# Reordering the first transfers and the first TensorE work of a one-core attention-and-MLP backward kernel, and leaving out fifteen marker loads

## The chip, the cores and the metric

The kernel runs on one core of one Trainium2 chip. The metric is the device time of one execution in microseconds (us). The time before is the median of three runs. A separate, profiled execution of the same program gives the profile and the trace.

A core has TensorE (PE, with its weight loads shown apart as PEld), VectorE (DVE), ScalarE (ACT), GpSimd (POOL) and SyncE (SP). SP issues nearly all transfers here. Transfers are carried out by 16 DMA engines that all queues share.

## The reference

The program computes one decode step of a block and its gradients, in bfloat16. `x` is one row of 640; there are 32 heads with a K and a V cache of 8192 x 128 each.

```
xn   = layernorm(x)
q    = xn @ wq                       # wq: 640 x 4096, 32 heads of 128
p    = softmax(q k^T / sqrt(128))    # per head, over 8192 keys
o    = p v
out  = x + concat(o) @ wo + (silu(xn @ w1) * (xn @ w3)) @ w2
# outputs: out, and for the cotangent grad_out the gradients of
# x, k_cache, v_cache, wq, wo, w1, w3, w2
```

Each head's K and V are 2 MB and are read once; their gradients, 2 MB each, are written once. That is 32 x 4 x 2 MB, nearly all of the traffic: the profile counts 303.56 MB in all.

## The kernel before, in words

**Tiles.** A head's K or V is one SBUF tile of 128 partitions x 8192 bf16 (16 KB per partition). There are ten such slots (`NSLOT`). The gradients of K and V are written in place, over K and V, by `outer` (L550), and stored from the same slot.

**Transfers.** `load_next` (L139) takes the next K or V from a list and issues its load on SP's queue; for head 0 through `fifo` (L105, an ordinary `dma_start`), afterwards through `fifo_wide` (L108). `store` (L563) issues a gradient's store on the same queue, appends the slot to the free list and calls `load_next`. After the start `lag` is 3, so that a load is issued only while three slots are on the free list. All of these are on one SP queue and are served in the order of issue.

**The weights in groups.** Four heads are a group. `load_wq` and `load_wo` (L117, L122) load a group's columns of wq and rows of wo, 640 KB each; `load_group` does both. Group 0 is loaded on SP's queue, the others on GpSimd's, where groups 1 and 2 are issued after heads 0 and 1. The MLP (`mlp`, L644) runs ahead of head 2 (`MLP_AT`) in four of the slots.

**The start.** SP issues wq of group 0, K of head 0, wo of group 0, V of head 0, K and V of head 1, then seven MLP weight loads, then K and V of head 2. The layer norm of x runs on the small engines meanwhile. Then, in TensorE's order: `prep_q` (L281), five products of xn with wq's chunks; `take_g` (L256), which spreads and broadcasts grad_out; `prep_qc` (L290), which turns the q row into columns; `first_half` (L305), which places head 0's q into the operand `qz`; and `T(0, "K", 0)`, `T(0, "K", 1)` (L400), the transposes of the first two of eight chunks of K. Each `T` is four transposes into a PSUM tile `pT` (three buffers) and one copy by ScalarE into a tile `KT` (four buffers, which also serve the two input rows and the q row).

**A head.** `head` (L834) goes on with the other transposes of K, each pair followed by `Mp` (L409), the products of an earlier pair with `qz`; then the same for V, the softmax, the weighted sums (`wsum`, L509) and the outer products of the head before. Instructions stand in written order on every engine (`manual_schedule`).

**The marker loads.** After the stores of heads 23 to 30 `store` issues a small load of n = 1 to 15 rows of 8 bytes into its own column of a tile `marks`, which nothing reads (L568 to L570):

```
n = 2 * (h - 23) + (kind == "K") + 1
if 1 <= n <= 15:
    fifo(marks[0:n, n - 1, :], x_rows[0:n, 0:4])
```

Of the kernel before, what the change touches and what calls it, by code (L numbers as in the profile page):

```python
# [9 lines left out]
BF16 = mybir.dt.bfloat16  # L10
# [11 lines left out]
def kernel(  # L22
# [22 lines left out]
    nc = tc.nc  # L45
# [14 lines left out]
    consts = ctx.enter_context(tc.tile_pool(name="consts", bufs=1))  # L60
# [44 lines left out]
    def fifo(out_, in_):  # L105
        nc.sync.dma_start(out_, in_)
# [10 lines left out]
    def load_wq(g, eng):  # L117
        wq_g = wpool.tile([P, NC, GW], BF16, name="wq_g", tag="wq_g")
        eng.dma_start(wq_g[:], wq_v[:, :, g * GW:(g + 1) * GW])
        grp[g] = dict(wq=wq_g)  # L120

    def load_wo(g, eng):  # L122
        wo_g = wpool.tile([P, GH, D], BF16, name="wo_g", tag="wo_g")
        eng.dma_start(wo_g[:], wo_v[:, g * GH:(g + 1) * GH, :])
        grp[g]["wo"] = wo_g

    def load_group(g, eng):
        load_wq(g, eng)
        load_wo(g, eng)

    x_rows = A_x.rearrange("a b (k w) -> (a b k) w", w=40)
    marks = consts.tile([16, 15, 4], BF16, name="marks")
    free_slots = [kvpool.tile([P, KVN], BF16, name=f"kv{i}", tag=f"kv{i}") for i in range(NSLOT)]
    kv_tiles = {}
    pending = [("K", h) if k == 0 else ("V", h) for h in range(H) for k in range(2)]
# [3 lines left out]
    def load_next():  # L139
        if not pending or len(free_slots) < lag[0]:  # L140
            return
        kind, h = pending.pop(0)
        t = free_slots.pop(0)
        (fifo if h == 0 else fifo_wide)(t[:], (kc if kind == "K" else vc)[h])
        kv_tiles[(kind, h)] = t

    load_wq(0, nc.sync)
    load_next()
    load_wo(0, nc.sync)
    for _ in range(3):  # L150
        load_next()
    mC = free_slots.pop(0)
# [71 lines left out]
    def kt_tile():  # L224
        return tpool.tile([P, 4, P], F32, name="KT", tag="KT")

    def t_tile():
        t = kt_tile()
        return t[:].rearrange("p k w -> p (k w)").bitcast(BF16)

    def pst():
        return ps_t.tile([P, 512], F32, name="pT", tag="pT")
# [6 lines left out]
    def spread(col, row):  # L239
        for ci in range(NC):  # L240
            nc.tensor.matmul(ps_xg[:, col + ci:col + ci + 1], lhsT=row.rearrange("o (p c) -> o c p", c=NC)[:, ci, :],
                             rhs=one_bf[0:1, :], start=True, stop=True)
# [13 lines left out]
    def take_g():  # L256
        spread(NC, g_row)
        nc.tensor.matmul(ps_xg[:, P:P + D - 512], lhsT=one_bf[0:1, :].to_broadcast([1, P]), rhs=g_row[:, 512:D],
                         start=True, stop=True)
        nc.tensor.matmul(ps_g[:], lhsT=one_bf[0:1, :].to_broadcast([1, P]), rhs=g_row[:, 0:512],  # L260
                         start=True, stop=True)
        nc.scalar.copy(g_bc[:, 0:512], ps_g[:])
        nc.scalar.copy(g_bc[:, 512:D], ps_xg[:, P:P + D - 512])
        nc.vector.tensor_copy(g_col[:], ps_xg[:, NC:2 * NC])

    def prep_new(g):
        G_ = grp[g]
        G_["cb"] = wpool.tile([P, 2, GH], BF16, name="cb", tag="cb")
        G_["do"] = wpool.tile([P, GH], F32, name="do_c", tag="do_c")
        G_["cm"] = wpool.tile([P, 2, 2, GH, 2], BF16, name="cm_g", tag="cm_g")  # L270
        G_["od"] = wpool.tile([P, GH, 2], F32, name="od_g", tag="od_g")
# [9 lines left out]
    def prep_q(g):  # L281
        G_ = grp[g]
        pq = pst()
        for ci in range(NC):
            nc.tensor.matmul(pq[:], lhsT=xn_col_bf[:, ci:ci + 1].to_broadcast([P, P]), rhs=G_["wq"][:, ci, :],
                             start=(ci == 0), stop=(ci == NC - 1))
        G_["qrow"] = t_tile()
        nc.scalar.activation(G_["qrow"][0:1, 0:GW], pq[0:1, :], ACTF.Copy, scale=scale)
# [16 lines left out]
    def first_half(a, ps, fresh):  # L305
        cb, cm = grp[0]["cb"], grp[0]["cm"]
        for par in range(2):
            for e in range(2):
                nc.tensor.matmul(ps[HW * e:HW * (e + 1), par * GH:(par + 1) * GH], lhsT=sel[:, par, :], rhs=cb[:, a, :],
                                 start=(fresh and par == 0), stop=True, skip_group_check=True)  # L310
        nc.vector.tensor_tensor(cm[:, :, a],
                                ps.rearrange("p (t h) -> p t h", t=2).unsqueeze(3).to_broadcast([P, 2, GH, 2]),
                                mask2.unsqueeze(1).unsqueeze(1).to_broadcast([P, 2, GH, 2]), ALU.mult)
        nc.vector.tensor_copy(
            hd[0]["qz"][:, QL:QL + 4 * QW].rearrange("p (a t n) -> p a t n", t=2, n=QW)[:, a, :, 0:2],
            cm[:, :, a, 0, :])
# [80 lines left out]
    def new_head(h):  # L397
        hd[h] = dict(kt={}, qz=qz_tiles[h % 2])

    def T(h, kind, c):  # L400
        W3 = kv_tiles[(kind, h)][:].bitcast(F32).rearrange("p (i w) -> p i w", w=P)
        pT = pst()
        for k in range(4):
            nc.tensor.transpose(pT[:, k * P:(k + 1) * P], W3[:, 4 * c + k, :], ident_f[:])  # L404
        KT = kt_tile()
        nc.scalar.copy(KT[:].rearrange("p k w -> p (k w)"), pT[:])  # L406
        hd[h]["kt"][(kind, c)] = KT
# [155 lines left out]
    def store(kind, h):  # L563
        t = kv_tiles.pop((kind, h))
        if kind == "K":
            hd.pop(h)
        fifo((dkc if kind == "K" else dvc)[h], t[:])
        n = 2 * (h - 23) + (kind == "K") + 1  # L568
        if 1 <= n <= 15:
            fifo(marks[0:n, n - 1, :], x_rows[0:n, 0:4])  # L570
        free_slots.append(t)
        load_next()

# [248 lines left out]
    def outers_a(h):  # L822
        outer_v(h, 0, J // 2)
        outer_v(h, J // 2, J)
        store("V", h)
        outer_k(h, 0, J // 2)

    def outers_b(h):
        outer_k(h, J // 2, J)
        store("K", h)  # L830
# [69 lines left out]

    prep_new(0)
    new_head(0)
    prep_q(0)
    take_g()
    ps_0 = pst()
    prep_qc(0, ps_0[:, 0:GH], True)
    first_half(0, ps_0[:, 8:8 + 2 * GH], False)
    T(0, "K", 0)
    T(0, "K", 1)
    for hh in range(GH):  # L910
        prep_do(0, hh)
    for h in range(H):
# [80 lines left out]
```

## Time and profile before

| what | value |
|---|---|
| time, median of 3 runs | 723.35 us (723.16 to 723.36) |
| the profiled execution's own time | 722.83 us |
| its span (first to last instruction) | 721.0 us |
| TensorE clock granted, mean | 0.928 |
| busy: PE, PEld, DVE, ACT, POOL | 602.1, 376.9, 472.2, 364.3, 85.1 us |
| DMA: bytes, mean rate | 303.56 MB, 421 GB/s |
| SP's queue: bytes, share of 16 engines | 276.39 MB, 90.1% |

The own time is 1.83 us above the span, and the median of the runs is 0.52 us above the own time. Busy shares are averages over stages that have different limits. The DMA share in a stretch is the mean of the 16 DMA engines; it counts a packet where it starts and so can pass 1.

### The profile page before, as it was taken

To read this page: it belongs to the slowest core of one execution; us is meant where nothing else is said; L and a number is where in the kernel's file an instruction comes from. 1 tells how busy PE (TensorE), PEld (TensorE's weight loads), DVE (VectorE), ACT (ScalarE), POOL (GpSimd) and SP (SyncE) were. 2 spreads that over 40 slices of the span, in tenths; PEclk is the share of its full clock that TensorE was granted. 3 is DMA by queue.
4 is the path that set the end of the run, shared out by engine and by line. 5 is a ranking of instruction groups with operands and counts; after the bars stand their busy time and mean duration, and the time that the engine had idled before them with its cause. 6 is when DMAs were issued, how large, how long until landed. Compare 5 with 4: busy or idle time off the path is not lost.

```text
span 721.0 us, 13243 instructions
## 1 busy us (share of the span) xinstructions
PE 602.1 (84%) x5237; PEld 376.9 (52%) x5244; DVE 472.2 (65%) x895; ACT 364.3 (51%) x726; POOL 85.1 (12%) x86
## 2 busy tenths in 40 slices
PE   6989699987999999878986899778987889978921
PEld 4556566645565556545553555445554555545510
DVE  4369927678858886767755765556774757667581
ACT  3641166653666566545554555455653556555510
POOL 0110100000101122111120111112210101111110
PEclk9987999997999999999998999899998999999965
DMA  9999999999999999999999999999999999999996
GB/s 358 400 418 413 437 428 424 425 436 428 420 425 422 431 429 428 418 434 431 423 423 430 423 430 427 423 429 430 430 419 430 427 432 427 428 432 425 424 428 295
DMA packets 23403, 303.56 MB, mean 421 GB/s; under 512 B 4054, under 2 KB 5404, under 8 KB 10156
## 3 DMA queue, kind: packets, MB, share of 16 engines
q1 hardware_dynamic: 16840, 276.39, 90.1%
q0 software_dynamic: 6496, 26.31, 9.1%
q8 instruction: 41, 0.67, 0.4%
q14 instruction: 22, 0.18, 0.1%
q10 hardware_dynamic: 4, 0.00, 0.0%
HBM read 151.34 MB, written 152.91 MB: 422 GB/s over the span
## 4 chain that ended last, share of the span: by engine, by line
DMA 45%; PE 39%; DVE 10%; ACT 3%; issue 2%; SPq 0%; ACTq 0%; DVEq 0%
DMA kv<-in_A_k_cache_dram 27%; PE pT L404 18%; DMA out_dram<-kv 13%; PE sA L425 5%; DVE kv L552 4%; PE dA L425 4%; PE X L519 4%; DMA kv<-in_A_v_cache_dram 3%; PE m L442 2%; ACT KT L406 2%; DMA out_dram<-rel,rel_idx 1%; PE gu_ps L649 1%; PE dh_ps L660 1%; PE dx_acc L747 1%; ACT KT L432 1%
## 5 line engine op out<-in xcount | busy, mean ns | idle before, releaser
L406 ACT COPY KT<-pT 128x512 f32<-128x512 f32 x512 | 288.2, 588 | 235.4 <-PE pT L404 214.8
L404 PE MATMUL pT<-ident_f,kv 128*128 128x128 f32 x2048 | 304.3, 287 | 53.9 <-DMA kv<-in_A_k_cache_dram 39.8
L404 PEld LDWEIGHTS pT<-ident_f,kv 128*128 128x128 f32 x2048 | 233.9, 147 | 144.2 <-PE pT L404 52.9
L552 DVE TENSOR_TENSOR kv<-qd,U 128x4096 bf16<-128x4096 bf16 x64 | 146.0, 2284 | 0.0
L552 DVE TENSOR_TENSOR kv<-qd,P 128x4096 bf16<-128x4096 bf16 x64 | 143.6, 2284 | 0.0
L519 PE MATMUL X<-kv,Z 128*32 128x512 bf16 x1024 | 96.8, 413 | 1.8 <-DVE Z L536 1.8
L425 PE MATMUL dA<-KT,qz 128*32 128x512 bf16 x512 | 84.9, 411 | 0.0
L425 PE MATMUL sA<-KT,qz 128*32 128x512 bf16 x512 | 82.0, 400 | 0.0
L372 POOL DMA_INDIRECT out_dram<-wq_g,row_idx x30 | 43.1, 1437 | 283.3 <-DMA out_dram<-wq_g,row_idx 108.0
L502 DVE SCALAR_TENSOR_TENSOR U<-m,P 128x64 bf16<-128x64 f32 x32 | 7.5, 235 | 94.3 <-PE m L442 94.3
L519 PEld LDWEIGHTS <-Z 128*32 128x32 bf16 x1024 | 32.7, 101 | 36.2 <-issue 9.4
L425 PEld LDWEIGHTS <-qz 128*32 128x32 bf16 x1024 | 29.5, 95 | 41.0 <-issue 38.1
L442 PEld LDWEIGHTS m<-selc,KT 64*128 64x128 f32 x256 | 21.1, 141 | 30.1 <-ACT KT L432 19.4
L442 PE MATMUL m<-selc,KT 64*128 64x64 f32 x256 | 30.0, 239 | 8.0 <-ACT KT L432 8.0
L468 DVE TENSOR_REDUCE mrow<-m 128x1 f32<-128x64 f32 x32 | 7.1, 223 | 41.7 <-PE m L442 41.4
L372 POOL DMA_INDIRECT out_dram<-rel,rel_idx x12 | 15.1, 1260 | 142.3 <-DVE rel L601 59.0
L462 ACT CAST qd<-pT 128x256 bf16<-128x256 f32 x32 | 11.9, 373 | 38.2 <-DVE kv L552 30.4
L475 DVE TENSOR_REDUCE negM<-m 128x1 f32<-128x128 f32 x32 | 9.3, 292 | 32.2 <-PE m L472 32.2
L276 DVE SCALAR_TENSOR_TENSOR side<-wo_g,g_bc 128x640 bf16<-128x640 bf16 x32 | 26.2, 819 | 2.3 <-DMA wo_g<-in_A_wo_dram 2.0
L607 DVE SCALAR_TENSOR_TENSOR wq_g<-wq_g,side 128x512 bf16<-128x512 bf16 x40 | 27.3, 683 | 0.0
L534 DVE SCALAR_TENSOR_TENSOR U<-m,P 128x128 bf16<-128x128 f32 x32 | 11.4, 355 | 15.5 <-PE m L532 15.5
L432 ACT COPY KT<-dA 64x512 f32<-64x512 f32 x32 | 18.6, 582 | 4.5 <-PE dA L425 4.5
(179 smaller groups left out, 403.9 us busy)
## 6 DMA issues: line engine op xcount, KB each, us to landing
out_dram<-kv SPq DMA_DIRECT2D x64, 2048.0 KB
kv<-in_A_k_cache_dram SPq DMA_DIRECT2D x32, 2048.0 KB
kv<-in_A_v_cache_dram SPq DMA_DIRECT2D x32, 2048.0 KB
out_dram<-wo_g POOLq DMA_DIRECT2D x8, 640.0 KB, 15.6
wq_g<-in_A_wq_dram POOLq DMA_DIRECT2D x7, 640.0 KB, 16.2
wo_g<-in_A_wo_dram POOLq DMA_DIRECT2D x7, 640.0 KB, 22.6
kv<-in_B_w_dram SPq DMA_DIRECT2D x2, 1728.0 KB
out_dram<-kv POOLq DMA_DIRECT2D x2, 1728.0 KB, 30.8
```

Source lines behind the costliest of these rows:

```text
L276: nc.vector.scalar_tensor_tensor(junk[:], G_["wo"][:, hh, :], 1.0, g_bc[:], ALU.mult, ALU.mult, accum_out=G_["do"][:, hh:hh + 1])
L372: nc.gpsimd.indirect_dma_start(dwq_row, bass.IndirectOffsetOnAxis(ap=idx, axis=0), src, None, element_offset=g * GW, bounds_check=(D - 1) ...
L404: nc.tensor.transpose(pT[:, k * P:(k + 1) * P], W3[:, 4 * c + k, :], ident_f[:])
L406: nc.scalar.copy(KT[:].rearrange("p k w -> p (k w)"), pT[:])
L425: nc.tensor.matmul(S_[kind][q:q + QW, :], lhsT=S_["qz"][:, o:o + QW], rhs=KTb[c][:, par, :], start=(c0 == 0 and par == 0), stop=(c0 == NCH ...
L432: nc.scalar.copy(XS[0:QH].rearrange("p k w -> p (k w)"), S_.pop(kind)[0:QH, :])
L442: nc.tensor.matmul(S_["m"][:, b0:b0 + 4 * J].rearrange("p (x c k t) -> p k x c t", x=4, k=4, t=2)[:, k], lhsT=XS[0:QH, k, :], rhs=selc[0:Q ...
L462: nc.scalar.copy(qd[:].rearrange("p a d -> p (a d)"), hd[h].pop("ps_r"))
L519: nc.tensor.matmul(xg["X"][q:q + QW, :], lhsT=Z[:, o:o + QW], rhs=W[:, N4 * i:N4 * (i + 1)], start=(slot == 0 and i < 4), stop=(slot == NS ...
L534: nc.vector.scalar_tensor_tensor(S_["U2"][:], S_["V"][:, 0:J].unsqueeze(2).to_broadcast([P, J, 2]), S_["m"][:, OC + NS:OC + NS + 1], S_["P ...
L552: nc.vector.tensor_tensor(dst[:, lo * DH:hi * DH].rearrange("p (j a b) -> p j a b", a=DH // 2, b=2), vec.rearrange("p (a b) -> p a b", b=2 ...
L607: nc.vector.scalar_tensor_tensor(wq_g[:, ci, :], wq_g[:, ci, :], 1.0, dqb, ALU.mult, ALU.mult, accum_out=dxa[:, ci, g:g + 1])
```

## The change

Three edits. K of head 0 is issued first, and then wq and wo of group 0 together. In TensorE's order `take_g` and the transposes of K's chunks 0 and 1 stand ahead of `prep_q`, `prep_qc` and `first_half`. The marker loads, their tile and their source view are gone.

```
-    x_rows = A_x.rearrange("a b (k w) -> (a b k) w", w=40)
-    marks = consts.tile([16, 15, 4], BF16, name="marks")
...
-    load_wq(0, nc.sync)
     load_next()
-    load_wo(0, nc.sync)
+    load_group(0, nc.sync)
     for _ in range(3):
         load_next()
...
         fifo((dkc if kind == "K" else dvc)[h], t[:])
-        n = 2 * (h - 23) + (kind == "K") + 1
-        if 1 <= n <= 15:
-            fifo(marks[0:n, n - 1, :], x_rows[0:n, 0:4])
         free_slots.append(t)
         load_next()
...
     prep_new(0)
     new_head(0)
+    take_g()
+    T(0, "K", 0)
+    T(0, "K", 1)
     prep_q(0)
-    take_g()
     ps_0 = pst()
     prep_qc(0, ps_0[:, 0:GH], True)
     first_half(0, ps_0[:, 8:8 + 2 * GH], False)
-    T(0, "K", 0)
-    T(0, "K", 1)
     for hh in range(GH):
         prep_do(0, hh)
```

More of the change, by code (lines that the diff above doesn't have):

```diff
@@ L129, in load_group @@
         load_wo(g, eng)
-    x_rows = A_x.rearrange("a b (k w) -> (a b k) w", w=40)
-    marks = consts.tile([16, 15, 4], BF16, name="marks")
     free_slots = [kvpool.tile([P, KVN], BF16, name=f"kv{i}", tag=f"kv{i}") for i in range(NSLOT)]
@@ L145, in load_next @@
         kv_tiles[(kind, h)] = t
-    load_wq(0, nc.sync)
     load_next()
-    load_wo(0, nc.sync)
+    load_group(0, nc.sync)
     for _ in range(3):
@@ L567, in store @@
         fifo((dkc if kind == "K" else dvc)[h], t[:])
-        n = 2 * (h - 23) + (kind == "K") + 1
-        if 1 <= n <= 15:
-            fifo(marks[0:n, n - 1, :], x_rows[0:n, 0:4])
         free_slots.append(t)
@@ L902 @@
     new_head(0)
+    take_g()
+    T(0, "K", 0)
+    T(0, "K", 1)
     prep_q(0)
-    take_g()
     ps_0 = pst()
@@ L907 @@
     first_half(0, ps_0[:, 8:8 + 2 * GH], False)
-    T(0, "K", 0)
-    T(0, "K", 1)
     for hh in range(GH):
```

## The prediction

> **What bounds the kernel now.** I read the page first, for the shares of the whole span.
>
> ```profile
> DMA  9999999999999999999999999999999999999996
> GB/s 358 400 418 413 437 428 424 425 436 428 420 425 422 431 429 428 418 434 431 423 423 430 423 430 427 423 429 430 430 419 430 427 432 427 428 432 425 424 428 295
> ...
> q1 hardware_dynamic: 16840, 276.39, 90.1%
> q0 software_dynamic: 6496, 26.31, 9.1%
> ```
>
> The 16 DMA engines are full in every slice but the last. The rate dips in the first slice and the last alone; between them it is 400 to 437 GB/s, whatever PE, DVE or ACT do. So the end is set by the transfers: when they start, how much the engines carry, and how evenly they finish. Windows over the start and the end show the two losses.
>
> ```profile
> 0.00:2.00 2.00, 0.00 (x0) 0.00 (x0) 0.98 (x8) 0.47 (x1) 0.70 (x6) 1.00 0.00 1
> 2.00:3.00 1.00, 0.36 (x6) 0.28 (x6) 0.80 (x4) 0.81 (x1) 0.00 (x0) 1.00 0.73 228
> 3.00:4.00 1.00, 0.58 (x2) 0.49 (x2) 0.35 (x3) 0.00 (x0) 0.00 (x0) 1.00 0.98 329
> ...
> 712.00:713.00 1.00, 0.00 (x0) 0.00 (x0) 0.00 (x0) 0.00 (x0) 0.00 (x0) 0.50 1.02 424
> 713.00:714.00 1.00, 0.00 (x0) 0.00 (x0) 0.00 (x0) 0.00 (x0) 0.00 (x0) 0.50 0.70 295
> 714.00:715.00 1.00, 0.00 (x0) 0.00 (x0) 0.00 (x0) 0.00 (x0) 0.00 (x0) 0.50 0.66 274
> 715.00:716.00 1.00, 0.00 (x0) 0.00 (x0) 0.00 (x0) 0.00 (x0) 0.00 (x0) 0.50 0.48 201
> 716.00:717.00 1.00, 0.00 (x0) 0.00 (x0) 0.00 (x0) 0.00 (x0) 0.00 (x0) 0.50 0.40 168
> 717.00:718.00 1.00, 0.00 (x0) 0.00 (x0) 0.00 (x0) 0.00 (x0) 0.00 (x0) 0.50 0.16 66
> 718.00:719.00 1.00, 0.00 (x0) 0.00 (x0) 0.00 (x0) 0.00 (x0) 0.00 (x0) 0.50 0.15 66
> ```
>
> The last two columns are the DMA share and GB/s. At the start nothing moves for 2 us; SP's first issue takes 0.68 us from 0.74. At the end no compute engine works after 710, and the share falls from full at 713 to 0.15, two to three engines, in the last stretch before 719. The engines do not finish together: the missing share adds up to 0.30+0.34+0.52+0.60+0.84+0.85 = 3.45 us that an even finish would save. The kernel's time is that of the last two or three engines.
>
> The third view is the timeline, of TensorE at the start and of SP where markers are issued; the fourth is SP's waits from 548 to 700 us.
>
> ```profile
> 6.67 2.29 PE L285 MATMUL pT<-wq_g,xn_col_bf 128*128 128x512 bf16 x5 [1.99 <-DMA wq_g<-in_A_wq_dram]
> ...
> 11.84 1.51 PE L404 MATMUL pT<-ident_f,kv 128*128 128x128 f32 x6 [0.85 <-DMA kv<-in_A_k_cache_dram]
> ```
>
> ```profile
> 570.66 0.58 SPq L106 DMA_DIRECT2D out_dram<-kv  x1
> 575.19 0.27 SPq L106 DMA_DIRECT2D marks<-in_A_x_dram  x1
> 580.13 0.48 SPq L111 DMA_DIRECT2D kv<-in_A_k_cache_dram  x1
> ```
>
> ```profile
> SPq L111 <- DMA out_dram<-kv: 67.7, 11, 10.8
> SPq L106 <- DMA kv<-in_A_v_cache_dram: 23.2, 6, 4.2
> SPq L106 <- DMA kv<-in_A_k_cache_dram: 19.2, 5, 4.0
> SPq L106 <- DMA out_dram<-kv: 18.6, 4, 4.8
> ```
>
> TensorE does q's products when wq has landed, and has 0.85 us idle before K. SP sits in front of a marker for 4 to 5 us until an older transfer has landed, then issues it; the load behind it waits for a store's landing anyway.
>
> **Part 1, the order of the first transfers.** K of head 0, wq and wo are 2.1, 0.65 and 0.65 MB whichever comes first, and SP makes the same three issues (0.68, 0.61, 0.42 us) ahead of V's: nothing behind them is issued later. First bytes come 0.07 us sooner, K's issue being the shorter. What can change is how evenly the engines leave this stage. The trace's landing events show it: wq lands from 13 engines at 4.70 to 5.17 us, from the other three at 6.28, 6.54 and 6.87. The packet records tell why: an engine's 1 KB packets take 0.046 us each until 4.3 us, but the last ones of the three late engines, beside K's 16 KB packets on the others, take 0.15 to 0.39. The same three offsets, 1.7 to 2.1 us, are there when K, wo, V and K of head 1 land (up to 23.5 us); later the spread grows to 5 to 8. With K first, late engines start as late, but run their wq beside wo on the others. The wo stage, run by late engines beside V's packets, added nothing to the offsets. So I expect most of the 1.3 us by which those three stand apart from the next to vanish: 3 x 1.3 / 16 = 0.25 us for the average engine. For the last engine the ends are -1.7 us (it is one of the three and its whole offset goes) and +2.5 us (rival 2). I take the average engine, -0.3 with the earlier first byte, since nothing ties the three to the last engines 700 us later.
>
> SP's ninth issue, the first large MLP weight, waits today for wq (1.0 us, issued at 7.0); it will wait for K, some 1 to 2 us longer. Four 2 MB transfers are queued ahead of it, so zero; without them it would cost that wait.
>
> **Part 2, the order on TensorE.** K lands at about 2.4 + 2.1 MB / 429 GB/s = 7.3 us plus up to 1.7 of straggling, so 7.5 to 9; the two `T` (8 of the 16 transposes that take 3.65 us at this point, 1.8 us) end by 9.3 to 10.8. wq lands where K lands now, 11.84, or up to 1.3 sooner. From wq to the end of `first_half` on PE is 6.67 to 10.98 today, 4.3 us; without `take_g` inside, whose ScalarE copies hold q's column copy, I estimate 3.8: 14.3 to 15.6. Chunks 2 and 3 of K, 8 transposes, follow at 1.8 us, so the first `Mp` comes at 16.1 to 17.4 instead of 15.41. One more wait is added: the four `KT` buffers turn by two places, chunk 3 falls on chunk 0's buffer, and ScalarE's copy of it waits for that `Mp` (0.79 us of PE); chunks 4 and on queue behind it on ScalarE, half a microsecond at most. So head 0 is later by 0.7 to 2.5 us; I take 1.8. It doesn't reach the end: V's store at 37.12 is queued behind loads that land up to 60 us. The thinnest cover that I found is the load issued at 124.05 us: it lands first at 133.3, and 2 MB take 4.9 us, so the engines reached it at 128.4, and 4.3 us of work stood before it. 1.8 is under 4.3: zero; if the cover were gone, +1.8.
>
> **Part 3, the markers.** Fifteen issues of 0.31 us and their waits leave SP, 4.6 us of issue in all. Their cover is the queue: a 2 MB load issued at 580.13 lands at 605.63, 25 us or five transfers later, so an SP that is 5 us sooner only makes the queue longer. Stores at the end come up to 5 us sooner (V of head 30's outer product ends at 676.8, its store is issued at 681.74) into a queue that lasts to 713. On the engines a marker's packet and its semaphore write take 0.012 to 0.015 us by the packet records: 0.2 us on an engine that has all fifteen, 0.1 on average, zero for one that has none. Windows agree: 429, 429 and 426 GB/s for 560 to 600, 600 to 640 and 640 to 680, against 427 from 300 to 548 without markers. I take -0.1.
>
> The Trainium skill, page "DMA: Bandwidth & Descriptors", section "Anatomy of one DMA", gives every transfer a fixed cost of about 2 us, most of it completion latency; were it paid by the engines, the fifteen would give back 30 us. The windows speak against that here: no share is missing beside a marker.
>
> **Sum.** 722.83 - 0.3 + 0 - 0.1 = 722.4 us for an execution like the profiled one; the median is 0.52 above it, so 722.9.
>
> **The rivals.** (1) The late three are the ones that end last. For it: the end is set by two or three engines, and in the early landings the same three gaps persist. Against: the spread changes by microseconds between 26 and 130 us. The end moves by 1.3 to 1.7, and the markers' 0.1 to 0.2 come on top: 723.35 - 1.7 = 721.7, and 721.5 at best. Chance 0.28.
>
> (2) Slower: wq in second place is slowed by 16 KB traffic. An engine has 40 packets of 1 KB; at 0.29 instead of 0.046 us each slow one costs 0.245. About seven were slow on a late engine. It passes 0.2% (1.45 us) from six more slow packets on an engine that ends last; with ten, 2.5 us: 725.8. For it: K's packets surround wq in time, and engines leave K at different moments. Against: those that leave first and are slowed are the early ones. Chance 0.18.
>
> The Trainium skill, same page, section "Latency and other measured facts", puts HBM latency at 0.2 us on average and 2 us at high load, which would slow every packet in second place; the packets of 0.046 and of 0.39 us lean that way.
>
> (3) Slower: head 0's delay is not absorbed, because an engine ahead of the others runs dry after the MLP: +1.8, 725.1. It decides when the delay passes 4.3 us. Chance 0.06.
>
> (4) The markers cost their issue time after all, 4.6 us: 718.7. Against: the windows. Chance 0.02.
>
> No measurable change, my forecast, keeps 0.46. 0.2% of 723.35 is 1.45 us, about what a measurement of this kernel can tell from no change. Faster by more is rivals 1 and 4, 0.30; slower by more is 2 and 3, 0.24. For the forecast alone the range is 721.9 to 724.3; to hold 8 in 10 it takes in rival 1 down to 721.0 and most of 3 and the lesser half of 2, up to 725.3.
>
> **What would show it.** In the profile after: wq lands after K, at 10.5 to 12 us; q's products start then; the first `Mp` is later by 1 to 2 us; the DMA share stays at 1 through 120 to 130 us; rates beside the former markers stay at 427 to 429; SP's loads and stores stand in pairs after 548 as they did before. I am wrong if the share falls at another time than from about 713 to 719, or if the landing spread of wq is over 3 us, or if a 20 us stretch between 100 and 700 us shows a share under 0.97.

## The result: slower by 0.2%, and the profile after

The changed kernel takes 724.76 us (median of 11 runs, 722.91 to 725.81) against 723.34 us for the kernel before beside it (11 runs, 722.66 to 724.24). The ratio is 1.0020, with a 95% interval of 1.0012 to 1.0027: slower by 1.4 us. The profiled execution took 724.07 us with a span of 722.3 us, 1.24 and 1.3 us more than before.

The page of the changed kernel, the same rows as were shown of before:

```profile
DMA  9999999999999999999999999999999999999996
GB/s 358 404 424 411 435 428 423 415 432 427 415 426 424 427 432 426 421 427 432 426 426 422 428 425 429 425 426 432 434 415 430 428 429 427 429 434 422 427 431 278
...
q1 hardware_dynamic: 16600, 276.39, 90.1%
q0 software_dynamic: 6496, 26.31, 9.1%
```

The bytes are the same, SP's queue has 240 packets fewer with the markers gone, and the 16 DMA engines are as full as before. The page doesn't show where 1.3 us went. The windows at the start and the end (last columns: DMA share, GB/s):

```profile
2.00:3.00 1.00, 0.36 (x6) 0.28 (x6) 0.80 (x4) 0.82 (x1) 0.00 (x0) 1.00 0.49 131
3.00:4.00 1.00, 0.58 (x2) 0.49 (x2) 0.35 (x3) 0.00 (x0) 0.00 (x0) 1.00 0.94 393
...
712.00:713.00 1.00, 0.00 (x0) 0.00 (x0) 0.00 (x0) 0.00 (x0) 0.00 (x0) 0.50 0.91 382
713.00:714.00 1.00, 0.00 (x0) 0.00 (x0) 0.00 (x0) 0.00 (x0) 0.00 (x0) 0.50 0.78 321
714.00:715.00 1.00, 0.00 (x0) 0.00 (x0) 0.00 (x0) 0.00 (x0) 0.00 (x0) 0.50 0.79 328
715.00:716.00 1.00, 0.00 (x0) 0.00 (x0) 0.00 (x0) 0.00 (x0) 0.00 (x0) 0.50 0.64 270
716.00:717.00 1.00, 0.00 (x0) 0.00 (x0) 0.00 (x0) 0.00 (x0) 0.00 (x0) 0.50 0.45 184
717.00:718.00 1.00, 0.00 (x0) 0.00 (x0) 0.00 (x0) 0.00 (x0) 0.00 (x0) 0.50 0.18 74
718.00:719.00 1.00, 0.00 (x0) 0.00 (x0) 0.00 (x0) 0.00 (x0) 0.00 (x0) 0.50 0.23 98
719.00:720.00 1.00, 0.00 (x0) 0.00 (x0) 0.00 (x0) 0.00 (x0) 0.00 (x0) 0.50 0.08 33
720.00:721.00 1.00, 0.00 (x0) 0.00 (x0) 0.00 (x0) 0.00 (x0) 0.00 (x0) 0.50 0.04 16
```

From 712 to 720 the missing share adds up to 0.09+0.22+0.21+0.36+0.55+0.82+0.77+0.92 = 3.94 us, against 3.45 before, from 713 to 719. The last packet ends at 720.68 us, before at 719.36. So in these two profiled executions about 0.5 of the 1.3 us is a less even finish. That the change makes the finish less even is not shown: counted on the packets from 700 us to the last one, the idle share is 3.48 us before and 4.11 after, and over the traces of all the kernels below it goes from 2.82 (e2_transfer_order, one of those that lose the most traffic) to 4.39 (e11_after_again), in no order of the traffic lost. The other 0.8 must have been lost earlier. The timeline of TensorE shows the start:

```profile
8.52 1.94 PE L401 MATMUL pT<-ident_f,kv 128*128 128x128 f32 x8 [0.85 <-DMA kv<-in_A_k_cache_dram]
11.84 2.29 PE L282 MATMUL pT<-wq_g,xn_col_bf 128*128 128x512 bf16 x5 [1.38 <-DMA wq_g<-in_A_wq_dram]
...
17.41 1.04 PE L422 MATMUL sA<-KT,qz 128*32 128x512 bf16 x4
18.38 1.36 PE L401 MATMUL pT<-ident_f,kv 128*128 128x128 f32 x8
```

The same two rows of the kernel before, the first `Mp` and the transposes behind it:

```profile
15.41 0.79 PE L425 MATMUL sA<-KT,qz 128*32 128x512 bf16 x4
16.14 1.10 PE L404 MATMUL pT<-ident_f,kv 128*128 128x128 f32 x8
```

K's first transposes now end before wq is there, TensorE waits 1.38 us, and the first `Mp` stands at 17.41 instead of 15.41. Half a microsecond more is added right there: this `Mp` takes 1.04 us instead of 0.79, and the eight transposes 1.36 instead of 1.10. What that does is seen 110 us later, in one window of each kernel. The first row is of before, the second of after:

```profile
124.00:140.00 16.00, 15.85 (x149) 9.78 (x145) 11.23 (x16) 10.94 (x23) 0.31 (x1) 1.00 1.02 432
```

```profile
124.00:140.00 16.00, 16.00 (x147) 10.12 (x138) 10.04 (x15) 10.37 (x21) 0.00 (x0) 1.00 1.03 419
```

The share is full in both; the rate is not. The engines are busy throughout, with packets that take longer. The packet records say which. The 64 packets of 32 KB of one load, K of head 6, take 1.23 us on average before and 1.41 after; 22 of them take over 1.3 us, up to 2.5. An extra 0.18 us for each of 64 packets, on 16 engines, is 0.7 us. SP's timeline has that load's issue, before and after:

```profile
124.05 0.47 SPq L111 DMA_DIRECT2D kv<-in_A_k_cache_dram  x1
```

```profile
125.58 0.47 SPq L111 DMA_DIRECT2D kv<-in_A_k_cache_dram  x1
```

Its first packet starts 3.6 us after the issue before, and 1.9 us after it in the changed kernel. In neither is an engine without work: at every moment from 124 to 140 us at least 16 packets are under way.

A running sum of all packets' bytes, as a difference from before divided by 428 GB/s, tells the rest: the changed kernel is 0.56 us ahead at 8 us, level from 12 to 24, 0.17 ahead at 128, 0.53 behind at 136 and 0.76 behind from 240 on. With the 0.5 us of the finish that is the 1.3 us.

### The profile page after: what moved, and what is told of

Its sections match the earlier page's. It is cut to its first block, busy times and chain, and to the rows that moved or that the text cites. A ratio compares the mean times of both kernels' runs of the same rounds, so it can differ in the third digit from the quotient of the medians.

```text
span 722.3 us, 13223 instructions
## 1 busy us (share of the span) xinstructions
PE 600.8 (83%) x5244; PEld 377.1 (52%) x5244; DVE 472.0 (65%) x895; ACT 364.0 (50%) x726; POOL 88.0 (12%) x86
## 4 chain that ended last, share of the span: by engine, by line
DMA 49%; PE 36%; DVE 9%; ACT 2%; issue 2%; SPq 0%; ACTq 0%; DVEq 0%
DMA out_dram<-kv 22%; PE pT L401 16%; DMA kv<-in_A_k_cache_dram 14%; DMA kv<-in_A_v_cache_dram 11%; PE sA L422 4%; DVE kv L549 4%; PE dA L422 4%; PE X L516 3%; PE m L439 2%; ACT KT L403 1%; DMA wq_g<-in_A_wq_dram 1%; PE gu_ps L643 1%; PE dh_ps L654 1%; PE pT L282 1%; PE dx_acc L741 1%
## 5 line engine op out<-in xcount | busy, mean ns | idle before, releaser
L516 PE MATMUL X<-kv,Z 128*32 128x512 bf16 x1024 | 94.6, 405 | 1.8 <-DVE Z L533 1.8
L422 PE MATMUL dA<-KT,qz 128*32 128x512 bf16 x512 | 83.4, 405 | 0.0
L369 POOL DMA_INDIRECT out_dram<-wq_g,row_idx x30 | 45.5, 1516 | 278.2 <-DMA out_dram<-wq_g,row_idx 73.7
```

The source lines that it names most:

```text
L369: nc.gpsimd.indirect_dma_start(dwq_row, bass.IndirectOffsetOnAxis(ap=idx, axis=0), src, None, element_offset=g * GW, bounds_check=(D - 1) ...
L422: nc.tensor.matmul(S_[kind][q:q + QW, :], lhsT=S_["qz"][:, o:o + QW], rhs=KTb[c][:, par, :], start=(c0 == 0 and par == 0), stop=(c0 == NCH ...
L516: nc.tensor.matmul(xg["X"][q:q + QW, :], lhsT=Z[:, o:o + QW], rhs=W[:, N4 * i:N4 * (i + 1)], start=(slot == 0 and i < 4), stop=(slot == NS ...
```

## The experiments

Fourteen kernels were run. Theory A, in the expectations, is that head 0's delay is passed on to the loads behind the MLP; each expectation spells out its rivals. "Issue" is the issue of K of head 6, "lead" the time from it to that load's first packet, "slow" counts those of its 64 packets that take over 1.3 us, GB/s is the window from 124 to 140 us, and "behind" the running sum at 300 us against before (negative: ahead). All of these are of the one profiled execution. Sorted by issue:

| kernel | issue | lead | slow | GB/s | behind | ratio to before, 95% interval |
|---|---|---|---|---|---|---|
| e13_store_order | 119.42 | 8.0 | 1 | 435 | -0.15 | 0.9997 (0.9988 to 1.0006) |
| e8_relocation | 123.77 | 3.8 | 1 | 438 | -0.11 | 0.9996 (0.9988 to 1.0005) |
| e9_mlp_later | 123.89 | 3.7 | 1 | 437 | -0.30 | 0.9997 (0.9988 to 1.0006) |
| before | 124.05 | 3.6 | 1 | 432 | 0 | 1 |
| e1_no_markers | 124.06 | 3.6 | 1 | 435 | 0.07 | 0.9996 (0.9987 to 1.0005) |
| e5_delay_5us | 124.23 | 3.2 | 1 | 437 | -0.25 | 1.0014 (1.0005 to 1.0024) |
| e7_k_first_caught_up | 124.80 | 2.6 | 4 | 429 | 0.15 | 1.0006 (0.9997 to 1.0014) |
| e11_after_again | 125.36 | 2.0 | 11 | 425 | 0.59 | 1.0027 (1.0015 to 1.0039) |
| e12_one_load_1us_later | 125.40 | 2.2 | 12 | 422 | 0.67 | 1.0005 (0.9994 to 1.0016) |
| after | 125.58 | 1.9 | 22 | 419 | 0.76 | 1.0020 (1.0012 to 1.0027) |
| e10_mlp_shorter | 125.95 | 1.5 | 21 | 415 | 0.89 | 1.0011 (0.9999 to 1.0023) |
| e6_delay_10us | 126.09 | 1.8 | 31 | 398 | 1.32 | 1.0024 (1.0015 to 1.0032) |
| e4_both_orders_markers_kept | 126.35 | 1.6 | 32 | 405 | 1.18 | 1.0022 (1.0013 to 1.0031) |
| e2_transfer_order | 126.79 | 1.5 | 37 | 390 | 1.76 | 1.0035 (1.0023 to 1.0047) |
| e3_tensor_order | 126.92 | 1.3 | 31 | 406 | 1.71 | 1.0013 (1.0004 to 1.0022) |
| e14_one_load_2us_later | 127.15 | 1.3 | 36 | 393 | 1.82 | 1.0020 (1.0011 to 1.0029) |

Two things stand behind the table. The traffic that a kernel loses from 128 to 136 us, by the running sum, is what the slow packets of K of head 6 take too long: 0.70 and 0.73 us in the changed kernel, 1.37 and 1.37 in e2, and within about 0.1 us in every row. And the lead of this one load is not the whole story. V of head 5, the load ahead of it, has leads of 3.7 to 3.9 us in e2, e3, e4 and e6; there 5 to 20 of its packets are slow (1.26 to 1.32 us on average), while K of head 6, at 3.6 to 3.8, has one slow packet in four other kernels.

### The parts of the change

**e1_no_markers**: the kernel before without the three places of the markers.

```
-    marks = consts.tile([16, 15, 4], BF16, name="marks")
...
-        if 1 <= n <= 15:
-            fifo(marks[0:n, n - 1, :], x_rows[0:n, 0:4])
```

> The kernel before, without the fifteen marker loads; nothing else is changed. Theory A (head 0 is later by 2.5 us, so that the loads after the MLP are issued later and the engines lose some 0.7 us on them near 130 us, and more at the uneven end): no change, within 0.3 us of before; the landing spread and the rates of the stretches stay. Theory B (the order of the first transfers leaves the engines uneven, whatever TensorE does): no change either. Theory C (the markers held SP back and so set how transfers stand in the queue at the end): 1.4 us slower than before.

Measured: 722.88 us, no difference that can be told; the interval has room for 0.9 us less and 0.4 us more. On SP the markers cost nothing that shows. On the engines the 240 packets that they need take 0.009 us each by the packet records, 0.14 us on the average engine.

**e2_transfer_order**: the kernel before with the new order of transfers alone.

```
-    load_wq(0, nc.sync)
     load_next()
-    load_wo(0, nc.sync)
+    load_group(0, nc.sync)
```

> The kernel before with the new order of the first transfers (K of head 0, wq, wo) alone: markers stay, q's products stand first on TensorE. q's products now wait for wq to about 11.8 us and all of K's transposes stand behind them, so the first product of K with q comes at about 19.8 us, 4.4 us later than before and 2.4 us later than in the changed kernel. Theory A: slower than before by 1.4 us or more. Theory B: slower by 1.4 us, as the changed kernel. Theory C: no change.

Measured: 725.78 us (median of six runs). q's products wait for wq until 12.19, and the first `Mp` comes at 20.04, 4.6 us later than before.

**e3_tensor_order**: the kernel before with the new order on TensorE alone.

```
+    take_g()
+    T(0, "K", 0)
+    T(0, "K", 1)
     prep_q(0)
```

> The kernel before with the new order on TensorE alone: grad_out's spread and K's first transposes ahead of q's products, while wq is still the first transfer. K lands at 11.8 us, and q's products wait behind its transposes: the first product of K with q comes at about 19.9 us, 4.5 us later than before. Theory A: slower than before by 1.4 us or more, with the loss in the stretch from 120 to 140 us or soon after. Theory B: no change, since the transfers stand as before. Theory C: no change.

Measured: 724.23 us. With the transfers in their old order K's transposes start at 11.85, when K has landed, and q's products, which began at 6.67 before, stand behind them until 13.61. The first `Mp` comes at 19.21, 3.8 us later. The loss, 1.1 us against before beside it, is less than the 1.4 expected, though head 0 is later than in the changed kernel.

**e4_both_orders_markers_kept**: both orders, with the markers.

> The changed kernel with the fifteen marker loads left in. Theories A and B: slower than before by 1.4 us, as the changed kernel. Theory C: no change against before.

Measured: 725.0 us. The two orders together make the whole loss; the markers have no part in it, by this and by e1.

### Delay by itself

**e5_delay_5us** and **e6_delay_10us**: the kernel before, with needless products of TensorE ahead of K's first transposes, 12 and 24.

```
+    ps_j = pst()
+    for _ in range(12):
+        nc.tensor.matmul(ps_j[:], lhsT=xn_col_bf[:, 0:1].to_broadcast([P, P]), rhs=grp[0]["wq"][:, 0, :],
+                         start=True, stop=True)
     T(0, "K", 0)
```

> The kernel before, all orders and markers as they were, with twelve needless products (128x512, xn with wq's first chunk, into a PSUM tile that nothing reads) on TensorE ahead of K's first transposes. By the 0.43 us of q's products they take some 5.1 us, of which 0.85 lie in the wait for K: head 0 is later by about 4.3 us, as in the two runs that changed one order each. Theory A (the delay alone does it): DMA loses 1.5 to 1.9 us between 100 and 140 us, the loads reached soon after their issue are slow there, and the time is 1.0 to 2.6 us above before. Theory B (the order of the first transfers does it): no change.

> The same with twenty-four needless products: head 0 is later by about 9.5 us. Theory A: the queue is dry for longer, so that the loss grows by more than in proportion, or by the delay beyond the 4.3 us of cover: 4 to 7 us above before. Theory B: no change.

Measured: 724.3 and 725.02 us. The first `Mp` is later by 1.75 and 4.9 us (17.16 and 20.35), not by the 4.3 and 9.5 expected. The products took 4.6 and 7.6 us (reckoned 5.1 and 10.2), and the sixteen transposes behind them ran faster than before:

```profile
15.30 1.94 PE L404 MATMUL pT<-ident_f,kv 128*128 128x128 f32 x16
```

This is e5; before, the same sixteen took 3.65 us from 11.84 on. A delay of head 0 alone, with the transfers in their old order, so costs about what the change costs: the intervals of the three overlap. In e6 most of the traffic is lost at the same place, 1.0 us from 128 to 136 us, and 0.4 before that, where V of head 5 is loaded. The profiled execution of e5 doesn't show a loss: at 722.31 us it is the shortest of its twelve, with a lead of 3.2 us; what the others lost was not seen.

**e7_k_first_caught_up**: the changed kernel, with all four first pairs of K's chunks ready before q's products (the q row in another tile), so that `Mp` can start at once.

```
     take_g()
-    T(0, "K", 0)
-    T(0, "K", 1)
+    for c in range(4):
+        T(0, "K", c)
     prep_q(0)
...
+    Mp(0, "K", 0)
```

> The changed kernel with head 0 brought back to its old time: all of the first four chunks of K are transposed while wq is on its way (the q row goes to another tile, so that four KT buffers are there), and the first product of K with q follows q at once, at about 16.2 us against 15.41 in the kernel before and 17.41 in the changed one. K stays the first transfer, no markers. Theory A: the loss between 100 and 140 us is gone but for a rest, and the time is within 0.5 us of before. Theory B: 1.4 us slower than before, like the changed kernel.

Measured: 723.89 us, between before and after, with an interval that includes no change. The first `Mp` came at 16.04, but the transposes behind it ran at a slower pace (eight in 1.97 us at 16.63, before in 1.10 at 16.14), and V's first store was still 2.0 us late (39.10 against 37.12; after: 39.65).

**e8_relocation**: e1 with another list of the blocks of wq's gradient rows that the kernel moves between partitions, which shifts a little work between DMA engines; a try at the uneven finish.

```
-    FROM = ((16, 48, 72, 76), (16, 48, 104, 84), (16, 48, 108, 116), (16, 48, 72, 84), (16, 48, 76, 80))
+    FROM = ((16, 48, 24, 76), (16, 48, 104, 24), (16, 48, 56, 116), (16, 48, 112, 84), (16, 48, 56, 80))
```

> An attempt to do better, beside the question: the kernel before without markers, with another table of the wq gradient's rows that are written from other partitions (FROM): three blocks of four rows each are taken off partitions 24 to 27 and 56 to 59, two off 112 to 115 or 56 to 59, instead of 72, 104, 108 and 76. By the markers of the kernel before, the engine that is seventh in their order lands 6.6 us after the first and the engines on 72 to 79 and 104 to 111 some 2.7 us; each block is 0.16 us in each of six groups, 1 us in all. If partitions and engines go together as I suppose, the last engine ends 1 to 2 us sooner: 721.5. If not, no change or up to 2 us slower. Theories A and B say nothing of it.

Measured: 722.9 us, the same as e1's 722.88. No gain.

### Which delay counts, and why

**e9_mlp_later** and **e10_mlp_shorter** take the start and the MLP apart. e9 is the kernel before with work added to the MLP; e10 is the changed kernel and leaves out four of the seven products of w1 for the gradient of x. The edits, in this order:

```
-            for ci in range(NA):
+            for ci in list(range(NA)) * (2 - wi):
                 nc.vector.tensor_scalar(wa[:, ci, :], bc_sb[:, wi, :], xn_col[:, ci:ci + 1], None, ALU.mult)
```

```
-            for f0 in range(0, F, FA):
+            for f0 in range(0 if wi else 4 * FA, F, FA):
```

> The kernel before, with nothing changed at the start; the four products that write the gradient of w1 in the MLP are written twice over (the same values), 2.4 us more of VectorE from 76.6 us on. Theory A (the time is lost behind the MLP: whatever makes the MLP's stores and the loads that wait for them 2.5 us later, lets these loads meet a nearly empty queue and move slowly): the loads behind the MLP are issued 1 to 3 us later, the mean 32 KB packet of one of them is 1.4 us or more instead of 1.23, the bytes moved by 240 us are 0.5 to 1.5 us behind the kernel before, and the median is 724.2 to 725.0. Rival B (the loss belongs to the start: the order of the first transfers, or head 0's place in it): 723.1, as before.

> The changed kernel, with four of the seven products of w1 for the gradient of x left out of the MLP (2.4 us of VectorE less; that part of the gradient of x is missing), so that the MLP's stores come at nearly the times that they have in the kernel before, while everything up to the MLP is as in the changed kernel. Theory A: the loads behind the MLP run as before (1.23 us a packet), the bytes are level with the kernel before at 240 us, and the median is 722.9 to 723.6. Rival B: 724.8, as the changed kernel.

Measured: 722.91 and 724.01 us. Theory A as I had worded it missed both: making w1's and w3's stores 2.5 us later cost nothing, and giving the 2.4 us back recovered nothing that the profile shows (415 GB/s); e10's interval holds both no change and the whole loss of the changed kernel. The timelines of GpSimd and SP suggest why. First e9, then e10: the store of w2, the store of w1, and the issue of the load (V of head 5) that waits for the latter's landing.

```profile
71.94 0.56 POOL L710 DMA_DIRECT2D out_dram<-kv  x1 [21.69 <-DVE kv L712]
...
81.75 0.56 POOL L751 DMA_DIRECT2D out_dram<-kv  x1 [8.14 <-DVE kv L750]
...
104.25 0.47 SPq L111 DMA_DIRECT2D kv<-in_A_v_cache_dram  x1
```

```profile
74.62 0.56 POOL L704 DMA_DIRECT2D out_dram<-kv  x1 [21.75 <-DVE kv L706]
...
79.70 0.56 POOL L745 DMA_DIRECT2D out_dram<-kv  x1 [3.41 <-DVE kv L744]
...
108.88 0.47 SPq L111 DMA_DIRECT2D kv<-in_A_v_cache_dram  x1
```

Before, these are 71.80, 79.29 and 104.63; after, 74.46, 81.95 and 108.70. The load follows the issue of w2's store, the first of seven on GpSimd's queue, and not that of w1's store, the one it waits for: the queue works off its 6480 KB in order until about 128 us, so what is issued into it at 80 or 82 us only waits longer. So head 0's delay seems to reach the loads through the moment at which this queue starts. In all sixteen traces the two go nearly in step, from 71.7 and 104.7 us (e1) to 77.8 and 114.2 (e6); no run moved w2's store by itself, so this link is argued and not shown.

**e11_after_again**: the changed kernel, unaltered.

> The changed kernel once more, on the same chip as the two others. Theory A: 724.3 to 725.2, and a second profile shows packets of 1.4 us or more in the loads behind the MLP, and bytes about 0.8 us behind from 140 us on. Rival B gives the same time; its profile would show the deficit by 20 us instead.

Measured: 725.01 us. The second profile ends nearly as far behind (0.59 us at 300), but only 0.3 us of it is lost from 128 to 136 us, with a mean packet of 1.30 us instead of the 1.4 expected; the rest goes between 150 and 220 us, where several loads with leads of 12 us and more have up to ten slow packets each. In the first profile 0.7 is lost at the place and 0.3 from 160 to 220. What costs traffic there stays open.

**e12_one_load_1us_later** and **e14_one_load_2us_later**: the kernel before, with a GpSimd fill in the slot of K of head 6 ahead of its load (1024 and 2560 columns). Nothing ahead of that load is changed.

```
+        if (kind, h) == ("K", 6):
+            nc.gpsimd.memset(t[:, 0:1024], 0.0)
         (fifo if h == 0 else fifo_wide)(t[:], (kc if kind == "K" else vc)[h])
```

> The kernel before, with one GpSimd fill of 1024 columns in the slot of K of head 6, ahead of that load (issued at 124.05 before): the load and what stands behind it on SP is issued about 1.1 us later, and nothing ahead of it moves. Theory L (a load that the engines reach within about 3 us of its issue moves slowly): its lead falls from 3.6 to about 2.5 us, its mean 32 KB packet rises from 1.23 to 1.3 to 1.45 us, the bytes fall 0.4 to 0.9 us behind at 128 to 136 us and stay there, and the median is 723.6 to 724.3. Rival M (the loss comes from something else that the order at the start brings, and the short lead only goes with it): 1.23 us a packet, 723.1.

> As e12_one_load_1us_later with 2560 columns: the load of K of head 6 is issued about 2.3 us later. Theory L: lead about 1.3 us, 1.45 us a packet or more, 1.0 to 2.0 us of traffic lost, median 724.2 to 725.2. Rival M: 723.1.

**e13_store_order**: the changed kernel, with the small store of w1's last rows behind w3's large one on GpSimd's queue, which frees that slot sooner.

```
             nc.gpsimd.dma_start(dv[:, 0:NA, :], wa)
+            if wi:
+                nc.gpsimd.dma_start(dw1_v[:, NA, :], w1b)
...
-            nc.gpsimd.dma_start(dv[:, NA, :], wb)
+            if wi:
+                nc.gpsimd.dma_start(dv[:, NA, :], wb)
```

> The changed kernel, with the small store of w1's last rows (432 KB) issued behind the large store of w3 on GpSimd's queue instead of ahead of it. The slot that K of head 6 waits for is so free some 2 to 3 us sooner, and everything up to 90 us is as in the changed kernel. Theory L: the lead of that load rises from 2.6 to 5 us, its packets take 1.23 us, no bytes are lost from 128 to 136 us, and the median is 722.9 to 723.6, level with the kernel before. Rival M: 724.8, as the changed kernel.

Measured: 723.64, 724.88 and 722.88 us. The issue and the window of e14, then of e13:

```profile
127.15 0.47 SPq L111 DMA_DIRECT2D kv<-in_A_k_cache_dram  x1
...
124.00:140.00 16.00, 16.00 (x151) 9.98 (x149) 11.61 (x18) 10.83 (x24) 2.23 (x1) 1.00 1.01 393
```

```profile
119.42 0.47 SPq L111 DMA_DIRECT2D kv<-in_A_k_cache_dram  x1
...
124.00:140.00 16.00, 16.00 (x144) 10.66 (x143) 10.74 (x15) 10.00 (x20) 0.00 (x0) 1.00 1.02 435
```

One load's issue, 3.1 us later in the kernel before, brings the loss of 1.8 us of traffic and 1.0020; the same load issued 6.2 us sooner in the changed kernel takes the loss away, with the start in the order that the change makes. That settles the cause of the traffic lost at 128 to 136 us. In e14 the slow packets of that load make up 1.3 us of what is lost there; a further 0.2 us is engines without work, up to five at a time, which the changed kernel does not have.

The start is not the same in every execution, though nothing in it is changed: V's first store comes at 37.12 before, at 37.47 in e14 and at 38.09 in e12, and in e13 w2's store comes at 73.74 against 74.46 after. So these single traces differ by up to a microsecond ahead of the load too; V of head 5 has no slow packet in any of the three, and the times of eleven runs each carry the verdicts. The leads in these three expectations were reckoned back from the first landing (2.6 in the changed kernel; 1.9 by the packets, which the table has). e12's traffic fell behind as expected, with 0.3 us of it from 128 to 136 and the rest later, but its interval includes no change.

e13 stands level with before (0.9997), and no kernel of the study is faster than before beyond its interval.

## Why the prediction was wrong

The forecast was 722.9 us and no measurable change; 724.76 lies in the range (721.0 to 725.3), but it is slower, 1.42 us above the kernel before beside it. I had taken 1.45 us for about what can be told from no change; eleven runs of each kernel tell more, with 1.0012 as the lower end of the interval.

**Part 2, "zero" for head 0's delay, is the step that failed.** Its sizes held: wq landed from 9.49 to 11.70 and TensorE took it at 11.84 (the landing times in the prediction are 0.24 us too late, the offsets between them hold), the first `Mp` at 17.41 is the upper end of 16.1 to 17.4, and the 2.0 us lie in 0.7 to 2.5. V's first store was 2.5 us later (39.65 against 37.12). I had also found the right place: the load issued at 124.05 is the one that decides. What failed is the rule that work ahead of the engines is cover down to zero. I put the cover at 4.3 us, reckoned back from the landing (by the packets it was 3.6), and let 1.8 us pass; only 1.5 us arrived there, no engine ran dry, and still 0.9 us of traffic was lost from 128 us on, 0.7 of it by 136. By the table the loss at K of head 6 begins between a lead of 3.2 and one of 2.6 us; the four kernels with the most traffic lost, up to 1.8 us, have leads of 1.3 to 1.8. It is no fixed border: V of head 5 was slow at 3.7 to 3.9.

So rival 3 (chance 0.06, 725.1) had the right chain, with the wrong point of decision: not an empty engine but a load that is issued too short a time before its turn. That its time was nearly right is luck. Its +1.8 is the whole delay of head 0, and what was measured is 0.8 us of lost traffic and, in the profiled execution, 0.5 us of finish.

**Part 1, -0.3 us, failed too.** The first packet did start sooner, at 1.77 us instead of 2.19, 0.4 us and not the 0.07 forecast, and the sum of bytes is 0.56 us ahead at 8 us. It is gone by 12 us. K's first twenty packets of 16 KB, issued 1.0 us before, took 1.15 us on average instead of 0.61, which is 0.7 us on the average engine. And wq now moves from 7 to 11 us, where windows from 8 to 12 us show 342 and 398 GB/s and before had 372 and 455; its 1 KB packets run at their own pace wherever they stand (0.046 us each, 356 GB/s on 16 engines; 329 GB/s from 3 to 4 us before). In second place they were neither helped nor hurt: the 640 packets took 2.14 us on the average engine, 2.21 before. The late engines' offsets were to shrink by 1.3 us; they stayed. wq lands with a spread of 2.21 us (before 2.17), and four engines instead of three stand apart by 1.41 to 2.21. Rivals 1 (the offset goes, 721.7) and 2 (wq is slowed and an offset grows, 725.8) fall with that, and e13, with K first and level with before, says the same of the order of transfers by itself. SP's issues behind the first three were later after all (K of head 1 at 5.69 us for 3.33), with 9.9 us of lead left.

**Part 3, -0.1 us for the markers, held** within what can be measured, and rival 4 (718.7) falls by e1. A marker's packet and the semaphore write behind it take 0.009 us each by the records, 0.018 together and so a little more than the 0.012 to 0.015 reckoned. The windows after give 429, 429 and 426 GB/s from 560 to 600, 640 and 680, as before, and SP's loads and stores stand in pairs.

```profile
581.51 0.48 SPq L111 DMA_DIRECT2D kv<-in_A_k_cache_dram  x1
582.03 0.58 SPq L106 DMA_DIRECT2D out_dram<-kv  x1
```

The Trainium skill, page "DMA: Bandwidth & Descriptors", section "Anatomy of one DMA", has about 2 us as a fixed cost of a transfer that GpSimd issues, most of it latency at the end. Fifteen small ones on SP's queue gave back nothing that can be told here (e1).

**My signs of being wrong were the wrong ones.** The share did not fall, the spread of wq stayed under 3 us, and no 20 us stretch went under 0.97. The share counts how long engines are busy, and slow packets keep it full; GB/s beside it, 419 for 432, showed the loss.

**What stays open.** Why the load moves slowly. It is not that 16 engines read at once: from 18 to 24 us, before, all 16 read 32 KB packets at 1.225 us and 429 GB/s. Nor are the first packets the slow ones in the changed kernel; thirteen of its 22 slow ones start from 131.4 to 133.0. Nor does the lead alone decide, as V of head 5 shows. Also open is why e2 costs more than e3 (intervals apart) with the same traffic behind at 300 us, what costs traffic from 150 to 220 us in some traces, and whether the 0.5 us of finish belongs to the change at all: no run took that by itself.

## What to carry to other kernels

Where transfers set the time, look for the load with the shortest time from its issue to its first packet, and count its cover as used up some microseconds before it is empty (three to four here). A delay at the start can cost its time a hundred microseconds later, at the one place where a queue is thin; here it went with the moment at which a backlogged queue started, not with the later issues into it. Moving a small store behind a large one on that queue was enough to undo the loss.

## What the hardware showed that I had not expected

A load that was issued 1.3 to 2.6 us before its turn moved slowly: 4 to 37 of its 64 packets of 32 KB took 1.3 to 3.2 us instead of 1.21. In the changed kernel, with a lead of 1.9 us, no engine waited for it. The Trainium skill, page "DMA: Bandwidth & Descriptors", section "Specifications", gives some 0.6 us to the first byte of a transfer that SP issues. A lead of 1.9 us is over that, and the load's first packet started at 127.45 us (before 127.69), but 22 of the 64 were slow all the same.

TensorE's pace at the start is not a matter of the time alone. Eight transposes took 1.97 us at 15.52 in the changed kernel, behind waits, and sixteen took 1.94 us at 15.30 in e5, right behind 4.6 us of products. What sets the pace no run here takes by itself.
